# Batch 0's k loaded from two issuing engines, and one tail store moved, in a fused linear-attention and feed-forward kernel

## The chip, the core and the metric

The kernel runs on one core of a Trainium2 chip. The core's engines run their own instruction streams side by side and wait for each other by semaphores. The profile names them PE (TensorE matmul; PEld is its weight load), DVE (VectorE), ACT (ScalarE), POOL (GpSimd) and SP (SyncE, which here only issues transfers). Transfers between HBM and the on-chip memory run on 16 DMA engines. An instruction on SP, ACT or POOL issues a transfer; the profile counts the packets of SyncE's queue as q1 (hardware) and those of POOL's as q0 (software).

The metric is the device time of one execution in microseconds (us), as the median of several runs. The profile is of one execution, and its span runs from the first to the last instruction.

## The reference

Eight batches, eight heads, 576 positions, head size 64, all float32. The first half is linear attention with cosine weights, the second a feed-forward layer on its output.

```python
pos = np.arange(S); theta = np.pi / 2.0 * pos / S
def phi(x, c, s):
    r = np.maximum(x, 0.0)
    return np.concatenate([r * c, r * s], axis=-1)
q_p, k_p = phi(q, cos_w, sin_w), phi(k, cos_w, sin_w)
kv = np.einsum('bhsf,bhsd->bhfd', k_p, v)
z = np.sum(k_p, axis=2)
num = np.einsum('bhsf,bhfd->bhsd', q_p, kv)
den = np.einsum('bhsf,bhf->bhs', q_p, z)[..., None] + 1e-06
attn = num / den
x = attn.transpose(0, 2, 1, 3).reshape(B * S, H * D)     # 4608 x 512
h = x @ w_in                                             # 512 x 2048
g = h * (1.0 / (1.0 + np.exp(-1.702 * h)))
out = g @ w_out                                          # 2048 x 512
```

## The kernel before

The order of every engine's instructions is the order in which the code is written; no scheduler moves them. Each of SP, ACT and POOL works through its own list, so a transfer that has to wait holds up what stands behind it on that engine.

**Start.** For batch 0 the tiles `kf` (k) and `qf` (q) are each loaded in two pieces, along the free dimension: 192 and 384 of the 576 columns of k, 256 and 320 of those of q (L61 to L63). With 128 partitions and four rows each, a piece of k is 512 runs, of 768 bytes in the first and 1536 bytes in the second. All four are issued by SP. POOL writes the index constants (L68 to L73), then copies one element of `kf`'s first piece into a small tile, the gate (L130). That copy has no use but to hold POOL until this piece is there; behind it POOL issues the loads of v as bf16 (`vb`, L132, two of them) and of the first two quarters of w_in (L124).

ACT begins with a table load, the sine and cosine weights (L89, L90) and a second table load with a trial of the gelu (L92). PE runs twelve matmuls on zeros (`idle`, L346) until there is work.

**From k to the feed-forward part.** `trig` (L142 on DVE, L140 on ACT) multiplies the positive part of a 64-column slice j by cosine and sine: two instructions a slice. In k, slices 0 and 1 go to DVE and 2 to ACT (these lie in the first piece); 6, 7, 8 to ACT and 3, 4, 5 to DVE (these lie in the second). Then follow: `ksum`, the sum over positions, on PE (L218); the same trig for q on DVE, ACT and one slice on POOL; turning q on PE (L171) and copying it out (L179, L181); `kv_mm`, the product of k and v (L207), copied out by `kv_evac` (L212); `num_mm` (L230) and its division `num_div` on DVE (L236, L238, L254); turning the quotient `xn` on PE (L274), copied out as `xT` by ACT (L280). With `xT` and `w_in` the first feed-forward matmuls run (L295, from `start_block`, L368).

**Steady state.** For each of eight batches: 64 matmuls of the first layer (L295) with gelu on ACT (L300), then 64 of the second (L332), with the attention of the next batch laid between. Its loads come from SP and POOL while the matmuls run.

**End.** The last 64 rows of each batch are gathered in four tail tiles, t = 4 to 7, each of two batches, and go through both layers at the end (`mm1_tails`, L312; `mm2`, L327). Within `mm2`, ACT copies a result to `ysb` (L336) and one or two stores send it out (L340): a tail tile takes two stores of 64 rows. `last` (L338) chooses the issuing engine. In the last batch, SP issues all but three: both of tile 4 and the first of tile 5 go by POOL.

Of the kernel before, what the change touches and what calls it, by code (L numbers as in the profile page):

```python
# [19 lines left out]
def kernel(  # L20
# [9 lines left out]
    nc = tc.nc  # L30
    B, H, S, D = q.shape
# [20 lines left out]
    def raw(name, dt=F32):  # L52
        return one.tile([128, NI, S], dt, name=name)

    def src_of(src, b, i0=0, i1=NI):
        return src[b, 2 * i0:2 * i1].rearrange("(i hh) (p j) d -> (hh p) i (j d)", hh=2, j=NS)

    qf = one.tile([128, 2560], F32, name="qf")
    kf, vf, vb = raw("kf"), raw("vf"), raw("vb", BF16)
    qf0 = qf[:, 0:NI * S].rearrange("p (i e) -> p i e", i=NI)  # L60
    for t, src, cut in ((kf, k, 192), (qf0, q, 256)):  # L61
        nc.sync.dma_start(out=t[:, :, 0:cut], in_=src_of(src, 0)[:, :, 0:cut])
        nc.sync.dma_start(out=t[:, :, cut:S], in_=src_of(src, 0)[:, :, cut:S])  # L63


    NP = NS + 5
# [251 lines left out]
    def rows(b, t):  # L318

        if t >= 4:  # L320
            return [(64 * u, 64, out_j[w][NS - 1] if w < 2 else out[(w + 1) * S - 64:(w + 1) * S])
                    for u, w in enumerate((2 * (t - 4), 2 * (t - 4) + 1))]
        if b < 2:
            return [(64 * u, 64, out_j[b][2 * t + u]) for u in range(2)]
        return [(0, 128, out[b * S:b * S + 512].rearrange("(p c) d -> c p d", c=4)[t])]

    def mm2(b, t, lo, hi, c0=0, c1=d_model):  # L327
        if lo == 0:
            yp[t, c0] = pmm.tile([128, d_model], F32, name="mm")
        for fc in range(lo, hi):  # L330
            w = gT[fc][:, ts(t, 128)] if t < 4 else gl_t[:, fc, ts(t - 4, 128)]
            nc.tensor.matmul(yp[t, c0][:, c0:c1], w, w_out_sb[:, fc, c0:c1],  # L332
                             start=(fc == 0), stop=(fc == FC - 1))
        if hi == FC:
            ysb = ypool.tile([128, d_model], F32, name="ysb")
            nc.scalar.activation(ysb[:, c0:c1], yp[t, c0][:, c0:c1], AF.Identity)  # L336
            for p0, n, dst in rows(b, t):
                last = b == B - 1 and t != 4 and (t, p0) != (5, 0)  # L338
                eng = nc.sync if last else nc.gpsimd
                eng.dma_start(out=dst[:, c0:c1], in_=ysb[p0:p0 + n, c0:c1])  # L340

# [116 lines left out]
    for t in range(4):  # L458
        mm2(0, t, 0, 4)
    mm2(0, 0, 4, 8)  # L460
    mm2(0, 1, 4, 8)
    ha = at_homes()
    qturn_pe(0, ha[0])
# [117 lines left out]
```

## Time and profile before

| what | us | from |
|---|---|---|
| median of 3 runs (292.34 to 292.56) | 292.51 | times |
| the profiled execution | 292.51 | times |
| its span | 290.8 | profile |
| k, first piece: issue, to landing | 0.79, 3.4 | transfers of `kf` |
| k, second piece: issue, to landing | 1.30, 4.8 | transfers of `kf` |
| q, first piece: issue, to landing | 1.83, 5.6 | transfers of `qf` |
| q, second piece: issue, to landing | 2.38, 7.0 | transfers of `qf` |
| v, first half: issue, to landing | 4.33, 6.2 | transfers of `vb` |
| w_in, first quarter: issue, to landing | 5.98, 10.2 | transfers of `w_in` |
| first feed-forward matmul (L295) starts | 16.20 | timeline |
| last ACT copy of a result ends | 288.04 | timeline |

The profile has a page of summaries (busy times, the chain of work that ended last, groups of instructions, transfers) and views that can be asked of one stretch of time. In a timeline a line has start, duration, engine, line of code, operation, tiles and shapes, and in brackets how long the engine stood before it and what ended that. In the chain of waits a line has start, duration and what was worked on or waited for. A window's line has the window, its length, the busy time of each engine with its instructions, the TensorE clock that was granted, the DMA engines' mean busy share and what they moved in GB/s. A queue's line has packets, MB and the time that its packets took, as a share of 16 engines.

### The profile page before, as it was taken

To read this page: it belongs to the slowest core of one execution; us is meant where nothing else is said; L and a number is where in the kernel's file an instruction comes from. 1 tells how busy PE (TensorE), PEld (TensorE's weight loads), DVE (VectorE), ACT (ScalarE), POOL (GpSimd) and SP (SyncE) were. 2 spreads that over 40 slices of the span, in tenths; PEclk is the share of its full clock that TensorE was granted. 3 is DMA by queue.
4 is the path that set the end of the run, shared out by engine and by line. 5 is a ranking of instruction groups with operands and counts; after the bars stand their busy time and mean duration, and the time that the engine had idled before them with its cause. 6 is when DMAs were issued, how large, how long until landed. Compare 5 with 4: busy or idle time off the path is not lost.

```text
span 290.8 us, 5789 instructions
## 1 busy us (share of the span) xinstructions
PE 284.3 (98%) x2330; PEld 154.8 (53%) x2330; DVE 124.1 (43%) x356; ACT 132.9 (46%) x232; POOL 37.8 (13%) x71
## 2 busy tenths in 40 slices
PE   7989999999999999999999999999999999999995
PEld 2775466755555554555455545554555455544444
DVE  4953645842648363826582567156624200000000
ACT  7957654693156214721463136412651167751111
POOL 6650044101210001001100110011000100002000
PEclk9999999999999999999999999999999999999999
DMA  7999999684689958975699469756975400002322
GB/s 250 244 214 287 372 267 363 172 181 128 126 225 306 220 132 276 260 197 145 225 277 227 122 192 335 184 143 152 379 94 74 117 36 3 0 0 44 87 88 72
DMA packets 67771, 52.48 MB, mean 180 GB/s; under 512 B 47969, under 2 KB 57953, under 8 KB 67745
## 3 DMA queue, kind: packets, MB, share of 16 engines
q1 hardware_dynamic: 60320, 32.52, 45.2%
q0 software_dynamic: 7424, 19.60, 23.6%
q8 instruction: 18, 0.29, 0.4%
q14 instruction: 9, 0.07, 0.1%
HBM read 36.70 MB, written 9.44 MB: 159 GB/s over the span
## 4 chain that ended last, share of the span: by engine, by line
PE 92%; DMA 5%; DVE 1%; POOL 1%; issue 0%; ACT 0%; ACTq 0%
PE mm L332 43%; PE mm L295 38%; PE mm L312 5%; DMA w_in<-in_moe_w_in_dram 3%; PE at L230 3%; PE at L207 3%; DMA kf<-in_k_dram 1%; PE at L171 1%; POOL vb L132 1%; DVE xn L254 0%; PE at L274 0%; DVE inv L238 0%; ACT ysb L336 0%; DVE den L236 0%; POOL gate L130 0%
## 5 line engine op out<-in xcount | busy, mean ns | idle before, releaser
L332 PE MATMUL mm<-w_out_sb,g 128*128 128x512 bf16 (+1 forms) x528 | 117.9, 373 | 0.0
L295 PE MATMUL mm<-xT,w_in 128*128 128x512 bf16 (+1 forms) x608 | 112.9, 345 | 0.2 <-DMA w_in<-in_moe_w_in_dram 0.2
L300 ACT ACTIVATE g<-mm 128x512 bf16<-128x512 f32 x128 | 75.1, 598 | 30.4 <-PE mm L295 30.2
L295 PEld LDWEIGHTS <-w_in 128*128 128x128 bf16 x608 | 61.6, 113 | 49.6 <-DMA w_in<-in_moe_w_in_dram 0.3
L332 PEld LDWEIGHTS <-g 128*128 128x128 bf16 x528 | 48.7, 97 | 49.6
L336 ACT ACTIVATE ysb<-mm 128x512 f32<-128x512 f32 (+1 forms) x37 | 21.7, 586 | 109.7 <-PE mm L332 106.7
L340 POOL DMA_DIRECT2D out_dram<-ysb x39 | 21.2, 547 | 205.6 <-ACT ysb L336 203.6
L142 DVE TENSOR_SCALAR kr<-kf,cosw 128x256 bf16<-128x256 f32 x64 | 22.5, 351 | 30.3 <-DMA kf<-in_k_dram 30.3
L254 DVE TENSOR_TENSOR xn<-at,inv 128x512 bf16<-128x512 f32 x40 | 27.7, 691 | 1.7 <-PE at L230 0.4
L142 DVE TENSOR_SCALAR kr<-kf,sinw 128x256 bf16<-128x256 f32 x64 | 22.6, 354 | 0.0
L236 DVE TENSOR_SCALAR den<-at 128x8 f32<-128x8 f32 x39 | 6.5, 166 | 34.4 <-PE at L230 34.4
L230 PEld LDWEIGHTS <-qT 128*128 128x128 bf16 x320 | 14.6, 97 | 8.1 <-issue 0.8
L212 DVE CAST kvs<-at 128x520 bf16<-128x520 f32 (+1 forms) x9 | 5.7, 635 | 28.9 <-PE at L207 28.9
L230 PE MATMUL at<-kvs,qT 128*128 128x65 bf16 x320 | 15.9, 193 | 0.7 <-ACT xT L280 0.7
L155 DVE TENSOR_SCALAR qn<-qf,sinw 128x512 bf16<-128x512 f32 (+1 forms) x30 | 14.4, 480 | 0.0
L155 DVE TENSOR_SCALAR qn<-qf,cosw 128x512 bf16<-128x512 f32 (+1 forms) x30 | 14.3, 476 | 0.0
L312 PE MATMUL mm<-xt,w_in 128*128 128x512 bf16 x64 | 14.0, 379 | 0.0
L332 PE MATMUL mm<-w_out_sb,gl_t 128*128 128x512 bf16 x64 | 14.0, 379 | 0.0
L313 ACT ACTIVATE gl_t<-mm 128x512 bf16<-128x512 f32 x16 | 9.6, 597 | 4.2 <-PE mm L312 4.2
L312 PEld LDWEIGHTS <-w_in 128*128 128x128 bf16 x64 | 7.2, 113 | 6.6
L207 PEld LDWEIGHTS <-kr 64*128 64x128 bf16 x576 | 9.3, 94 | 2.7 <-issue 2.5
L332 PEld LDWEIGHTS <-gl_t 128*128 128x128 bf16 x64 | 6.3, 98 | 7.5
(63 smaller groups left out, 115.4 us busy)
## 6 DMA issues: line engine op xcount, KB each, us to landing
kf<-in_k_dram SPq DMA_DIRECT2D x5, 1152.0 KB, 6.9
vf<-in_v_dram SPq DMA_DIRECT2D x5, 1152.0 KB, 9.6
qf<-in_q_dram SPq DMA_DIRECT2D x5, 1024.0 KB, 6.2
out_dram<-ysb POOLq DMA_DIRECT2D x20, 256.0 KB, 2.8
out_dram<-ysb POOLq DMA_DIRECT2D x19, 128.0 KB, 4.1
kf<-in_k_dram POOLq DMA_DIRECT2D x2, 1152.0 KB, 11.7
vf<-in_v_dram POOLq DMA_DIRECT2D x2, 1152.0 KB, 16.5
w_in<-in_moe_w_in_dram POOLq DMA_DIRECT2D x4, 512.0 KB, 10.2
```

What stands on the lines that cost most here:

```text
L142: eng.tensor_scalar(o, i, 0.0, w[:, j:j + 1], op0=MAX, op1=MUL)
L155: nc.vector.tensor_scalar(o, i, 0.0, sc, op0=MAX, op1=MUL)
L207: nc.tensor.matmul(st["kv", i][:, hh, ds(col, n)], kr[r, j, i, :], rhs(r, i, j), start=(j == 0), stop=(j == NS - 1))
L230: nc.tensor.matmul(ps[:, h // 4, ds((h % 4) * 65, 65)], qT[:, h, ts(c, 128)], st["kvs"][:, hh, i, 0:65], start=True, stop=True)
L254: nc.vector.tensor_tensor(xn, pv[:, :, :, 0:64], inv.unsqueeze(3).to_broadcast([128, 2, 4, 64]), op=MUL)
L295: nc.tensor.matmul(hp[fc][:, t0:t1], w_in_of(kc, fc), x[b][:, kc, t0:t1], start=(kc == 0), stop=(kc == KC - 1))
L300: nc.scalar.activation(g, hp.pop(fc), AF.Gelu_apprx_sigmoid)
L312: nc.tensor.matmul(hps, w_in_of(kc, fc), xt[:, kc, :], start=(kc == 0), stop=(kc == KC - 1))
L313: nc.scalar.activation(gl_t[:, fc, :], hps, AF.Gelu_apprx_sigmoid)
L332: nc.tensor.matmul(yp[t, c0][:, c0:c1], w, w_out_sb[:, fc, c0:c1], start=(fc == 0), stop=(fc == FC - 1))
L336: nc.scalar.activation(ysb[:, c0:c1], yp[t, c0][:, c0:c1], AF.Identity)
L340: eng.dma_start(out=dst[:, c0:c1], in_=ysb[p0:p0 + n, c0:c1])
```

## The change

Two edits. The loop that loads k and q of batch 0 has an engine beside each pair: the second piece of k is issued by ScalarE (ACT), where it stands ahead of the first table load in that engine's list; the second piece of q and both first pieces stay on SP. And the condition for the stores of the last batch loses its exception, so the first store of tail tile 5 is issued by SP and no longer by POOL. PE and DVE have the same instructions as before, in the same order.

```diff
-    for t, src, cut in ((kf, k, 192), (qf0, q, 256)):
+    for t, src, cut, eng in ((kf, k, 192, nc.scalar), (qf0, q, 256, nc.sync)):
         nc.sync.dma_start(out=t[:, :, 0:cut], in_=src_of(src, 0)[:, :, 0:cut])
-        nc.sync.dma_start(out=t[:, :, cut:S], in_=src_of(src, 0)[:, :, cut:S])
+        eng.dma_start(out=t[:, :, cut:S], in_=src_of(src, 0)[:, :, cut:S])
...
-                last = b == B - 1 and t != 4 and (t, p0) != (5, 0)
+                last = b == B - 1 and t != 4
                 eng = nc.sync if last else nc.gpsimd
                 eng.dma_start(out=dst[:, c0:c1], in_=ysb[p0:p0 + n, c0:c1])
```

## The prediction

> **What bounds the kernel now.** I read the page's busy times first, then the chain of waits in order of time, then the timeline of the first 20 us, then the transfers in short windows.
>
> ```profile
> span 290.8 us, 5789 instructions
> ...
> PE 284.3 (98%) x2330; PEld 154.8 (53%) x2330; DVE 124.1 (43%) x356; ACT 132.9 (46%) x232; POOL 37.8 (13%) x71
> ```
>
> PE is busy for 98% of the span, so time can be won or lost only where PE does filler (the warm-up matmuls of L346) or stands: in the first 19 us, and after the last matmul. The chain of waits shows what the start hangs on:
>
> ```profile
> 4.21 0.18 POOL gate L130
> 4.38 1.59 POOL vb L132 x2
> 5.98 10.17 DMA w_in<-in_moe_w_in_dram
> ```
>
> Ahead of these the chain has k's first piece (L62, on SyncE's queue, issued 0.79, landed 4.16). The first real matmul of the feed-forward part (L295) starts at 16.20, when the first w_in tile has landed. But it has a second condition that came almost as late. The timeline (start, duration, engine):
>
> ```profile
> 4.26 0.35 DVE L142 TENSOR_SCALAR kr<-kf,cosw 128x256 bf16<-128x256 f32 x1 [2.15 <-DMA kf<-in_k_dram]
> ...
> 5.26 0.34 DVE L142 TENSOR_SCALAR kr<-kf,sinw 128x256 bf16<-128x256 f32 x1
> ...
> 6.12 0.51 ACT L140 ACTIVATE kr<-kf,cosw 128x256 bf16<-128x256 f32 x1 [0.97 <-DMA kf<-in_k_dram]
> 6.12 0.35 DVE L142 TENSOR_SCALAR kr<-kf,cosw 128x256 bf16<-128x256 f32 x1 [0.52 <-DMA kf<-in_k_dram]
> ...
> 15.65 0.39 PE L274 MATMUL at<-ident,xn 128*128 128x128 bf16 x4
> ...
> 16.20 1.09 PE L295 MATMUL mm<-xT,w_in 128*128 128x128 bf16 x16 [0.16 <-DMA w_in<-in_moe_w_in_dram]
> ```
>
> PE had ended its turn of xn at 16.04 and stood 0.16 us. So two chains race: the arithmetic from k to xT (16.04) and the w_in load (16.2). DVE uses k's first piece for four operations from 4.26 to 5.60, stands 0.52, and from 6.12, when the second piece is there, is busy almost without a gap until 13.2, each result feeding the next. ACT has the same shape with a gap of 0.97.
>
> The windows (columns: window, its length, busy of PE, PEld, DVE, ACT, POOL, clock, DMA share, GB/s) say how k came:
>
> ```profile
> 1.90:2.40 0.50, 0.50 (x2) 0.15 (x1) 0.12 (x2) 0.49 (x3) 0.38 (x1) 1.00 0.81 72
> 2.40:2.90 0.50, 0.50 (x2) 0.15 (x1) 0.00 (x0) 0.48 (x2) 0.00 (x0) 1.00 0.68 152
> 2.90:4.20 1.30, 1.30 (x4) 0.44 (x3) 0.00 (x0) 1.10 (x2) 0.00 (x0) 1.00 1.09 385
> 4.20:6.10 1.90, 1.77 (x19) 0.93 (x17) 1.34 (x4) 0.91 (x2) 1.89 (x4) 1.00 1.07 396
> 6.10:8.60 2.50, 1.80 (x26) 1.12 (x25) 2.48 (x9) 2.48 (x7) 1.42 (x2) 1.00 1.08 390
> 8.60:16.20 7.60, 6.64 (x158) 5.19 (x157) 6.75 (x21) 5.98 (x13) 6.49 (x9) 1.00 1.23 209
> ```
>
> After a slow first microsecond SyncE's queue alone keeps all 16 DMA engines full, 385 to 396 GB/s, until k and q (2.36 MB) are through at 8.6. Adding up the rates, k's first 393 kB had passed by 3.63 and landed at 4.16, all 1180 kB by 5.63, landed 6.1: about half a microsecond from last byte to release.
>
> **The change, part by part.**
>
> *ScalarE issues k's second piece.* SP's issues of the kind took 0.46 to 0.51 us here (one later k load 1.52). It stands ahead of ACT's first table load, which so moves from 0.79 to about 1.28; cosw, ready at 2.50 now, is ready near 3.0 (4.0 at the longest issue), and nothing asks for it before k lands at 4.16. ACT's own start on k moves from 4.24 to 4.5, covered by the later landing below. Cost nothing; without that cover, 0.5.
>
> *SP issues q 0.5 us earlier* (1.83 to 1.30, 2.38 to 1.83). Worth nothing by itself: the DMA engines are full until 8.6, and the order of bytes decides.
>
> *k's two pieces are now asked for at the same time.* This is the step that costs. Today they come one after the other: every packet before 3.0 is of 768 bytes, the first piece's. From two queues they can take turns. The nearest rows are POOL's queue (q0) beside SyncE's (q1), first in 8.5 to 9.0, then in 88 to 89 (packets, MB, share):
>
> ```profile
> q0 software_dynamic: 65, 0.07, 86.6%
> q1 hardware_dynamic: 59, 0.06, 34.5%
> ```
> ```profile
> q1 hardware_dynamic: 88, 0.20, 51.1%
> q0 software_dynamic: 71, 0.20, 50.9%
> ```
>
> When both run, they alternate nearly packet for packet. Each piece of k is 128 x 4 = 512 packets (768 and 1536 bytes), so taking turns both end together, with the whole 1180 kB: the first piece lands at 6.1 instead of 4.16, the second at 6.1 as now. DVE then does ten kr operations from 6.1 where it did six from 6.12. The first four take 1.34 (4.26 to 5.60), so today's work is as if ten had started at 6.12 - 1.34 = 4.78: DVE's chain is late by 1.32. ACT's shift is smaller (its first two took 0.91). DVE's stream stays packed, so xT is late by the same; minus the 0.16 in which PE now waits for w_in: +1.16. If the turns go by bytes instead, the first piece lands at 5.15 and the second, sharing with q's first piece, at 7.1: DVE late by 0.98, sum +0.82. If ACT's piece goes wholly first, DVE, which takes the first piece first, is as late as with turns.
>
> What could be won is the slow first microsecond: 112 kB moved between 1.9 and 2.9 where 390 could. No row shows two queues starting at once. Bounds: no gain, or the whole start-up, 0.7 us; I take 0.3, as if each queue starts at the row's rate (224 kB instead of 112). Both landings are then 5.8, DVE late by 1.02, PE by 0.86.
>
> [...]
>
> *What follows POOL's gate.* The gate (L130) waits for k's first piece, so vb and w_in are issued some 1.6 us later: vb near 6.0, w_in at 7.6. Cover: those bytes could not move anyway. vb was issued at 4.33 and two packets of POOL's queue passed before 8.5, when q was through; a POOL store near the end had its first packet 1.1 us after its issue (264.34 to 265.45). Issued at 6.0, vb is ready at 7.1, before 8.3 to 8.6. From there the queue runs without a gap at about 209 GB/s, so w_in lands at 16.15 or 0.3 sooner. Without the cover the cost is a rival below. The late POOL trig of q (L142) has 1.6 us to spare before its turn at 13.6.
>
> *The tail store.* The first store of tile 5 moves from POOL (0.53 us at 267.8) to SP, where one more issue of 0.33 to 0.59 ends near 268.5; SP's next store is ready at 270.96. Its semaphore wait is for a transfer of the stage before, long landed. The end hangs on the last ACT copy at 287.66 and its store: nothing; without the 2.4 us of cover, 0.5.
>
> **Sum.** Profiled execution: 292.51, its span 290.8 and 1.7 around it; the median of the runs is the same 292.51. 292.51 + 0.86 = 293.4. PE is full from 19 us on, so nothing later gives it back. The likeliest case's own range is 292.9 (0.7 of start-up won) to 293.7 (none).
>
> **Rivals.**
> 1. *The first piece still goes first; not slower.* For it: a queue with work in hand is not interrupted. vb waited from 4.33 to 8.4, and a POOL store issued at 82.58 behind a k load of 80.63 landed only after 6.5 us. If SP's packets are at the DMA engines first, k lands at 4.16 and 6.1 as now: 292.5. If the start-up is also 0.3 to 0.5 shorter, DVE's 0.52 gap closes, w_in follows as q drains earlier, and PE starts up to 0.5 sooner: 292.0. It decides as soon as the first piece lands before 4.78 while the second is no later than 6.1. Against it: both issues leave at about 0.79, so neither has work in hand.
> 2. *The w_in load becomes the bound.* If the 10.17 us from issue to landing were latency that moves with the gate, w_in would land 1.6 to 1.9 later and PE with it: 294.1 to 294.4. Against it: the empty POOL queue until 8.4.
> 3. *The second queue changes nothing:* ScalarE's issue comes first in its program, but if its packets only join when SP's first piece is through, the order of bytes is the old one and the time is 292.5. Against it: SP's own issue had packets 1.1 us later (0.79 to 1.9), and ACT stood free from 0.79 as well.
>
> **How the numbers follow.** Taking turns, or ScalarE's piece first: 0.62, of it 0.55 slower than 0.2% (0.585 us; about what a measurement of this kernel can tell from no change) and 0.07 within. First piece first: 0.25, of it 0.15 within and 0.10 faster. w_in: 0.08, slower. The rest 0.05, spread 0.02 faster, 0.02 within, 0.01 slower. That makes 0.12 faster, 0.24 the same, 0.64 slower. Range 292.1 to 294.0: it takes in most of rival 1 and the upper end of the turns, and leaves out the best of rival 1 and rival 2.
>
> **What would show it.** Right: k's first piece lands at 5 to 6.1; DVE's first kr operation starts there, without a gap before its fifth; the gap of PE before L295 is put down to the xn turn, not to w_in; w_in's time from issue to landing shrinks from 10.2 to below 9; L295 starts near 17.1. Wrong: a first piece at 4.2 (rival 1), POOL's queue standing idle after 8.6 (rival 2), or PE gaps behind the tail.

## The result, and the profile after

The changed kernel takes 294.68 us as the median of 6 runs (293.62 to 294.99), the kernel before 292.36 (292.22 to 292.56, 6 runs): a ratio of 1.007, 95% interval 1.0059 to 1.0081, or 2.3 us more. Its runs fall into two groups with nothing between: four at 294.64 to 294.99, in which TensorE's mean granted clock is 0.992 to 0.994, and two at 293.62 and 293.66 with a clock of 1.000. The median lies in the first group. The profiled execution (294.72, span 293.0) is one of the first group.

The heads of the page, TensorE's clock in 40 slices of the span, and two lines of the chain of waits:

```profile
span 293.0 us, 5752 instructions
...
PE 283.2 (97%) x2294; PEld 155.3 (53%) x2330; DVE 124.6 (43%) x356; ACT 132.8 (45%) x232; POOL 37.1 (13%) x70
...
PEclk9799999999999999999999999999999999999998
```
```profile
0.79 4.93 DMA kf<-in_k_dram
5.83 2.13 DVE kr L142 x6
```

k's first piece now lands 4.93 us after its issue, not 3.4, and DVE's work on it has entered the chain that ended last. In the timeline, lines that answer to those of the prediction, and the matmul that PE waited to start:

```profile
5.78 0.18 POOL L130 COPY gate<-kf 1x1 f32<-1x1 f32 x1 [3.50 <-DMA kf<-in_k_dram]
5.81 0.51 ACT L140 ACTIVATE kr<-kf,cosw 128x256 bf16<-128x256 f32 x1 [1.29 <-DMA kf<-in_k_dram]
5.83 0.35 DVE L142 TENSOR_SCALAR kr<-kf,cosw 128x256 bf16<-128x256 f32 x1 [3.71 <-DMA kf<-in_k_dram]
...
6.50 0.25 PE L218 MATMUL mm<-sel,kr 128*128 128x2 bf16 x4 [0.78 <-DVE kr L142]
...
7.22 0.35 PE L218 MATMUL mm<-sel,kr 128*128 128x2 bf16 x8 [0.47 <-DVE kr L142]
...
8.63 0.59 PE L346 MATMUL mm<-warm 128*128 128x512 bf16 x1
...
14.08 1.02 ACT L179 ACTIVATE qT<-mm 128x1024 bf16<-128x1024 bf16 x1 [1.77 <-PE mm L171]
...
14.26 0.17 DVE L236 TENSOR_SCALAR den<-mm 128x8 f32<-128x8 f32 x1 [0.55 <-PE mm L244]
...
17.99 1.06 PE L295 MATMUL mm<-xT,w_in 128*128 128x128 bf16 x16
```

Three things are to be seen. DVE has no gap before its fifth operation any more; it starts 1.57 us later (5.83 for 4.26). PE stands in two long pieces at 5.7 to 7.2, and from 8.2 on its matmuls are longer (a filler on zeros takes 0.59 us where it took 0.38). And DVE and ACT, which led PE before, now wait for it; the chain of waits runs through PE's work from 8.0 on, where before it ran through the w_in load. The windows show the clock that was granted:

```profile
8.00:8.20 0.20, 0.20 (x5) 0.20 (x6) 0.20 (x1) 0.20 (x1) 0.20 (x1) 0.93 1.03 384
8.20:8.40 0.20, 0.20 (x4) 0.01 (x1) 0.20 (x2) 0.20 (x2) 0.20 (x2) 0.50 1.05 390
...
11.20:11.40 0.20, 0.20 (x4) 0.20 (x3) 0.20 (x2) 0.20 (x1) 0.20 (x1) 0.50 1.24 213
11.40:11.60 0.20, 0.20 (x5) 0.20 (x4) 0.20 (x1) 0.20 (x2) 0.20 (x1) 0.54 1.22 203
```

It is 0.50 from about 8.17 to 11.58, 3.4 us (worked out from the two mixed windows, 0.93 and 0.54).

L295 starts 1.79 us later than before, and that delay is carried unchanged to the end: the last ACT copy ends at 289.81 for 288.04, 1.77 later. The span, however, is 2.2 longer. From the last ACT copy to the end it now takes 3.19 us, before 2.76 (spans are given to 0.1 us), though the last store lands 1.8 us after its issue in both. So there are two places to explain, the first 18 us and the last 3.

### The profile page after: what moved, and what is told of

The parts are those of the page before. It is cut to its first block, busy times and chain, and to the rows that moved or that the text cites. A ratio compares the mean times of both kernels' runs of the same rounds, so it can differ in the third digit from the quotient of the medians.

```text
span 293.0 us, 5752 instructions
## 1 busy us (share of the span) xinstructions
PE 283.2 (97%) x2294; PEld 155.3 (53%) x2330; DVE 124.6 (43%) x356; ACT 132.8 (45%) x232; POOL 37.1 (13%) x70
## 4 chain that ended last, share of the span: by engine, by line
PE 93%; DVE 2%; DMA 2%; ACT 2%; issue 1%; ACTq 0%; DVEq 0%
PE mm L332 42%; PE mm L295 36%; PE mm L312 5%; PE at L207 3%; PE at L230 3%; DMA kf<-in_k_dram 2%; ACT g L300 1%; PE mm L346 1%; PE mm L171 1%; DVE kr L142 1%; DVE xn L254 1%; PE at L171 1%; PE at L274 1%; PE mm L218 0%; ACT xT L280 0%
## 5 line engine op out<-in xcount | busy, mean ns | idle before, releaser
L332 PE MATMUL mm<-w_out_sb,g 128*128 128x512 bf16 (+1 forms) x505 | 116.2, 372 | 1.4 <-issue 0.3
L295 PE MATMUL mm<-xT,w_in 128*128 128x512 bf16 (+1 forms) x599 | 112.4, 345 | 0.5
L295 PEld LDWEIGHTS <-w_in 128*128 128x128 bf16 x608 | 61.7, 113 | 49.3
L340 POOL DMA_DIRECT2D out_dram<-ysb x38 | 20.4, 538 | 203.5 <-ACT ysb L336 203.4
L142 DVE TENSOR_SCALAR kr<-kf,sinw 128x256 bf16<-128x256 f32 x64 | 22.0, 345 | 0.0
```

Source lines behind the costliest of these rows:

```text
L142: eng.tensor_scalar(o, i, 0.0, w[:, j:j + 1], op0=MAX, op1=MUL)
L295: nc.tensor.matmul(hp[fc][:, t0:t1], w_in_of(kc, fc), x[b][:, kc, t0:t1], start=(kc == 0), stop=(kc == KC - 1))
```

## The experiments

All times are medians, with the kernel before run beside them on the same chip (292.29 in the first set, 292.30 in the second, 292.53 in the third).

**act_only: the first edit alone.**

```diff
-                last = b == B - 1 and t != 4
+                last = b == B - 1 and t != 4 and (t, p0) != (5, 0)
```

> Only the first edit: k's second piece on ScalarE's queue; the first store of tile 5 goes by POOL as before. If the whole loss comes from the first edit, the time is that of the change: about 293.6 where the clock stays at 1.000 and 294.6 to 295.0 where it drops to half near 8 us, and the span ends about 1.4 us after the last store has landed (1.36 in the change, 0.9 before). If the tail store on SP makes the longer end, the span ends 0.9 us after the last landing again and both times are 0.4 lower.

Measured: 293.24, ratio 1.0041 (1.0024 to 1.0058). Six runs at 293.09 to 293.36 with a clock of 0.998 to 1.000, two at 294.30 and 294.94 with 0.993 and 0.994. The last copy ends at 290.48 of a span of 293.2: 2.7 us, as before. The first of the two expectations, that all loss is in the first edit, was wrong; the second held for the undisturbed runs. What stays is +0.9 in the undisturbed runs and more where the clock drops.

**tail_only: the second edit alone** (the exception for tile 5 taken out of the kernel before).

> Only the second edit: the first store of tile 5 on SP, all loads as before. If the tail store costs nothing: 292.4, ratio 1.000, the span ends 0.9 us after the last landing. If it makes the longer end of the change: 292.8, ending 1.4 us after it.

Measured: 292.66, ratio 1.0016 (1.0008 to 1.0025), and 3.2 us from the last copy to the end. The times are 0.37 above the kernel before. The one store, which should have cost nothing, makes the longer end.

**act_store: the same store by ScalarE in place of POOL, loads as before.**

```diff
-                eng = nc.sync if last else nc.gpsimd
+                eng = nc.sync if last else nc.scalar if b == B - 1 and (t, p0) == (5, 0) else nc.gpsimd
```

> The kernel before with one difference: the first store of tile 5 is issued by ScalarE (near 267.5) in place of POOL. Loads and start as before. If the mere use of a second hardware queue costs time at the end of the execution: the span is 0.3 to 0.5 longer, 292.8, and it ends about 1.4 us after the last landing, L295 first at 16.2. If the longer end belongs to the start of the change or is chance: 292.4, ending 0.9 us after the last landing.

Measured: 292.75, ratio 1.0017 (1.0006 to 1.0028), 3.19 us from the last copy to the end. (L295 starts at 16.70 in this profile and not at 16.2; the six profiles with the old loads and the old fillers have it anywhere from 15.84 to 16.70.) By itself the longer end looks like a price of the second queue, but act_only uses that queue and ends in 2.7. What tail_only, act_store and the change share is one more transfer on the hardware queues (SP's and ScalarE's together). act_only has as many as before. In the built program each such transfer gets one of eight completion semaphores in turn, and a store first waits for the earlier transfer on its own. The last store of the kernel before, and of the change:

```
95 L340 DMACopy out_dram<-ysb 128x256 [waits DMAHW7_49,Activation_49]
95 L340 DMACopy out_dram<-ysb 128x256 [waits DMAHW0_49,Activation_49]
```

One transfer more moves the last store from the last of the eight semaphores to the first. The built program ends, behind the last store, with SyncE waiting for the eight one after the other, 0 first and 7 last (L576). The trace has these waits. From the last landing until SyncE goes on, the kernel before has one left, the change eight:

```profile
L576 SPq EVENT_SEMAPHORE  x1: 28/28/28, 289.9 to 289.9; - x1
```
```profile
L576 SPq EVENT_SEMAPHORE  x8: 28/28/28, 291.7 to 292.1; - x8
```

The seven more start some 0.06 us apart, 0.4 us in all.

**end_mid, end_six, end_one: the last store on other semaphores,** by moving tail stores between SP and POOL in the kernel before.

```diff
-                last = b == B - 1 and t != 4 and (t, p0) != (5, 0)
+                last = b == B - 1 and t not in (4, 5, 6) and (t, p0) != (7, 0)   # end_mid
+                last = b == B - 1 and t not in (4, 5)                            # end_six
+                last = b == B - 1 and (t, p0) != (4, 0)                          # end_one
```

> The kernel before with four more tail stores issued by POOL: both of tile 5, both of tile 6 and the first of tile 7. The number of transfers on the hardware queues falls by four, so with eight completion semaphores given out in turn the last store of all sits on the fourth (index 3) and not on the last (index 7). If the end of the program waits for the eight in order, each after the last landing costing its share, the span ends 2.74 + 4/7 x 0.45 = 3.0 us after the last ACT copy, time 292.55. If only index 7 is short, 3.2. If what matters is that POOL issues the store, or that SP issues one more, it stays at 2.75 or gets shorter: 292.3.

> The kernel before with one more tail store by POOL (the second of tile 5), so the last store of all sits on index 6 of the eight semaphores. If each semaphore still to be asked after the last landing costs about 0.06 us: from the last ACT copy to the end of the span 2.8 (index 7 gave 2.72 to 2.76, index 3 3.08, index 0 3.17 to 3.20). If the order of asking is another one, anything up to 3.2.

> The kernel before with two more tail stores by SP (the first of tile 5, the second of tile 4), so the last store of all sits on index 1. If the semaphores are asked in order: 3.1 to 3.15 from the last ACT copy to the end of the span, a little under the 3.2 of index 0. If the end grows with the number of stores that SP issues: more than 3.2.

From the last ACT copy to the end of the span (spans are given to 0.1 us):

| index of the last store's semaphore | SyncE's waits from the last landing on | us | kernels |
|---|---|---|---|
| 7 | 1 | 2.72 to 2.76 | before, act_only, act_fill, no_fill, same_order |
| 6 | 2 | 2.81 | end_six |
| 3 | 5 | 3.08 | end_mid |
| 1 | 7 | 3.15 | end_one |
| 0 | 8 | 3.17 to 3.20 | the change, tail_only, act_store, after_fill |

The end shortens as the index rises, whichever engine issues the moved stores and however many SP issues. After the last landing the program still waits for that store's semaphore and for the later ones, one after the other, some 0.06 us each. (end_mid was expected at 3.0.) The times of these three kernels (end_mid 292.61, 1.0013, 1.0001 to 1.0024; end_six 292.34, 0.9995, 0.9983 to 1.0006; end_one 292.68, 1.0002, 0.9986 to 1.0018) are too coarse to show such steps.

**after_fill: the change with more filler at the start.**

```diff
-    w = idle(12)
+    w = idle(18)
```

> The change with 18 warm-up matmuls on zeros in place of 12, so PE is busy until about 7.0 us and not 5.7. If PE's stand between 5.7 and 8 us is what halves its clock, and the clock what parts the runs of 294.7 from those of 293.6: clock 1.000 in every run, all times 293.5 to 293.8, L295 first near 16.9 to 17.1. If the clock drops for another reason (the DMA or DVE load of the first 8 us), times are as in the change, 293.6 to 295.0 in two groups. If the six added matmuls (about 1.3 us) hold up the sum of k: a still later L295, above 18.

Measured: 293.65, ratio 1.0047 (1.0035 to 1.0059); six runs at 293.56 to 293.87, clock 0.997 to 1.000, L295 at 16.82. The stretch from 5.7 to 8.2 us in the change (first line) and with the filler (second):

```profile
5.70:8.20 2.50, 1.06 (x19) 0.66 (x19) 2.38 (x7) 2.39 (x6) 2.42 (x4) 0.99 1.08 390
```
```profile
5.70:8.20 2.50, 2.50 (x26) 1.24 (x24) 2.50 (x8) 2.50 (x7) 2.50 (x4) 1.00 1.07 388
```

DVE, ACT and the DMA engines do nearly the same in both; PE is busy for 1.06 us of the 2.5 in the one, for all of it in the other. With six useless matmuls more, no run has the clock of 0.992 to 0.994. L295 starts 1.17 us earlier than in the change's profile; a part of that is not the clock, since in this execution k's first piece also landed 0.3 us earlier (DVE starts on it at 5.54, not 5.83).

**act_fill: the first edit alone, with the filler.** Both edits above together.

> The first edit alone (the first store of tile 5 by POOL as before) with 18 warm-up matmuls in place of 12. If the loss is three separate things (start +0.9, clock drop in some runs, end +0.45), only the first is left: clock 1.000 in every run, 293.2, all runs within 0.4, and the span ends 2.75 us after the last ACT copy as before. If the long end goes with the fuller start or with ScalarE's queue: 293.6, 3.2 us after the last copy.

Measured: 293.42, ratio 1.0039 (1.0024 to 1.0053), all five runs at 293.35 to 293.50, 2.73 us from the last copy to the end, L295 at 17.07. In act_only's profile, which is of a run at 0.994, DVE starts on k's first piece at 5.79, here at 5.78; L295 starts there at 18.34, 1.27 later, with a clock of 0.50 from 9.66 on. What is left here is the cost of the late first piece by itself, 1.1 us; without the filler act_only's undisturbed runs gave 0.9. Whether the longer filler costs the 0.2 between them stays open.

**no_fill: the kernel before without the fillers between the sums of k.**

```diff
     for j in (3, 6, 4, 7, 5):
-        idle(1, w)
         ksum(j)
-    idle(1, w)
     ksum(8)
```

> The kernel before without the six filler matmuls between the sums of k (zeros on zeros, no result). Loads as before. If PE's stand in the window from 5.7 to 9 us is enough to halve the clock: clock below 1.000 in some or all runs, and those about 0.5 to 1.2 us longer, 292.8 to 293.5, the rest 292.3. If the clock drops only together with the change's loads: clock 1.000 throughout and 292.2 to 292.3.

Measured: 293.50, ratio 1.0041 (1.0026 to 1.0056), all four runs at 293.39 to 293.64 with a clock of 0.994. k lands as before (3.4 and 4.9 us after issue), yet L295 starts at 17.25:

```profile
9.20:9.40 0.20, 0.20 (x6) 0.16 (x4) 0.19 (x2) 0.20 (x1) 0.00 (x0) 0.75 1.24 213
9.40:12.40 3.00, 2.78 (x47) 2.24 (x48) 2.76 (x6) 2.50 (x7) 2.60 (x4) 0.50 1.22 206
...
12.60:12.80 0.20, 0.20 (x8) 0.13 (x3) 0.00 (x0) 0.00 (x0) 0.20 (x1) 0.72 1.32 220
```

The same 3.4 us at a clock of 0.50, with the old loads. So the drop needs nothing of the change but the thinner work on PE, and it costs 1.2 us here.

**same_order: both queues, the old order of bytes.**

```diff
-    for t, src, cut in ((kf, k, 192), (qf0, q, 256)):
-        nc.sync.dma_start(out=t[:, :, 0:cut], in_=src_of(src, 0)[:, :, 0:cut])
-        nc.sync.dma_start(out=t[:, :, cut:S], in_=src_of(src, 0)[:, :, cut:S])
+    for c0, c1 in ((0, 192), (192, S)):
+        for i0, eng in ((0, nc.sync), (2, nc.scalar)):
+            eng.dma_start(out=kf[:, i0:i0 + 2, c0:c1], in_=src_of(k, 0, i0, i0 + 2)[:, :, c0:c1])
+    for c0, c1 in ((0, 256), (256, S)):
+        nc.sync.dma_start(out=qf0[:, :, c0:c1], in_=src_of(q, 0)[:, :, c0:c1])
...
-                last = b == B - 1 and t != 4 and (t, p0) != (5, 0)
+                last = b == B - 1 and t not in (4, 5) and (t, p0) != (6, 0)
```

> The kernel before with k cut over the two queues another way: SP and ScalarE each load one half of the rows of the first piece, then each one half of the second; q on SP as before; two tail stores go from SP to POOL so that the last store keeps its semaphore (index 7). Both queues now carry the bytes in the old order. If taking turns between the pieces is what made the first one late: all of the first piece lands at 4.0 to 4.3, L295 starts at 16.0 to 16.3, time 292.2 to 292.5. If using a second queue makes the loads slow by itself: first piece after 5, time 293 or more. If two queues shorten the start-up by the 0.3 that the prediction took: first piece near 3.9, time 292.0.

Measured: 292.70, ratio 1.0013 (1.0004 to 1.0023). All of the first piece is there at about 4.1 (DVE starts at 4.19), the second near 6.3, L295 at 16.46. ScalarE's queue carries half of each piece, and the first piece is on time; so the order of the bytes is what made it late. From 2 to 4 us this kernel moved 174 and 375 GB/s, where one queue moved 138 and 386 (means of 2 to 3 and 3 to 4 us): 0.02 MB more, or 0.06 us. Two queues shorten the start-up by next to nothing. The time is 0.2 above what was expected for this case. What the 0.4 us above the kernel before consists of stays open; L295 is 0.26 later, which is inside the 15.84 to 16.70 of the six profiles with the old loads and fillers.

## Why the prediction was wrong

The direction was right and the step that was priced came out near its price, in part by luck. The time was too low because of two steps that failed: the prediction had no price for what PE's stand does to TensorE's clock (measured: 1.2 us in the runs where it dropped), and it priced the moved tail store at nothing (0.4). Without the drop of the clock the time is 293.64 (the two runs at a clock of 1.000), inside the range of 292.1 to 294.0; with it, outside.

**k's first piece, taking turns: right in the end, its size by errors that cancelled.** Forecast: landing at 5.8, +0.86. Measured: landing at 5.72, DVE from 5.83, +0.9 (act_only, undisturbed runs) to +1.1 (act_fill). The queues did take turns, but not from the start (q1 is SP's, q10 ScalarE's; first 2 to 3 us, then 3 to 4):

```profile
q1 hardware_dynamic: 153, 0.12, 66.1%
q10 hardware_dynamic: 4, 0.01, 1.6%
```
```profile
q10 hardware_dynamic: 135, 0.21, 57.7%
q1 hardware_dynamic: 192, 0.15, 45.0%
```

Both transfers were issued at 0.79, yet ScalarE's queue had moved 4 packets by 3.0, when SP's had moved 160 of the 512 of the first piece. That head start, which the forecast did not have, brought the first piece forward; then the turns favoured the small packets (192 to 135), and from 4 to 5 us they were nearly even (165 to 178). Why ScalarE's queue starts later stays open. It is also why the 0.3 us of start-up that the forecast took off did not come: the change moved 124 and 355 GB/s from 2 to 4 us, less than the 138 and 386 of one queue. The landing lies between the two bounds, by packets (6.1) and by bytes (5.15). The second piece landed at 6.46, not 5.8, and no engine had to wait for it: DVE asked for it at 7.08, ACT at 6.62.

**ScalarE's issue, free: right.** It took 0.47; the cosine weights were ready at 3.01, long before 5.72.

**POOL's gate, hidden: right.** v and w_in were issued 1.6 us later, as forecast, and w_in landed 7.3 us after its issue, at 14.9. Rival 2 is out. L295 waited for xT. That w_in came earlier than the 16.15 of the profile before is not shown to be the change's doing: with the old loads it landed 8.5 to 8.6 us after its issue, at 14.5 to 14.7, in end_mid, end_six and end_one, and L295 did not wait for it there. The close race of two chains that the prediction read was that of one execution.

**The tail store, free: wrong.** The prediction looked at the store's issue and at the wait ahead of it, not at what follows the last landing. One transfer more on the hardware queues moved the last store from semaphore 7 to 0, and the span ends 0.43 later. In times: 293.64 (the change's two runs at 1.000) less 293.2 (act_only's) is 0.4; tail_only has 0.37 alone.

**PE's stand, priced at nothing: wrong, and the largest term.** The prediction saw that time can be lost where PE does filler or stands, but it reckoned only how late the work comes. Before, the sums of k and the fillers between them followed the warm-up matmuls almost at once, and PE was busy for 1.80 of the 2.5 us from 5.7 to 8.2:

```profile
5.70:8.20 2.50, 1.80 (x29) 1.10 (x29) 2.08 (x7) 2.08 (x6) 1.82 (x3) 1.00 1.08 391
```

In the change it was busy for 1.06, and in four of six runs the mean clock fell (0.992 to 0.994); the profile of one of them shows 0.50 for 3.4 us, and in it DVE and ACT wait for PE's sums and turns. That costs 1.2 (294.8 less 293.64), as no_fill does without the change.

It strikes only some runs, six of fourteen of the change and act_only. In the three profiles with a drop (the change, act_only, no_fill) the clock falls to 0.50 at 8.17, 9.66 and 9.30, each time for 3.413 us, and falls again after PE's last matmul, in each 283.306 us after the first fall; that is 83 times 3.4133. In the kernel before, the warm-up matmuls start 0.43 us apart up to 4.21 and 0.22 apart from there (the profile gives the clock as 1.00 all along), and from 4.20 to the clock's fall at 290.918 it is 286.72 us, 84 times 3.4133. An estimate from these distances: in these executions the clock changed only at steps of 3.413 us, which lay differently against the start of the kernel in each. That this is what parts the runs is not shown, since only one run of each kernel has a trace.

The sum, then: 0.9 for the late first piece, 0.4 at the end, 1.2 for the clock in four of six runs, together 2.5; those four lie 2.3 to 2.6 above the kernel before.

## What to carry to other kernels

Where one queue already fills the DMA engines (386 to 402 GB/s from 3 to 8 us here), a second one added no bandwidth (355 to 395). It only changed the order of the bytes, and a piece that was cut small to arrive early lost its place. The six filler matmuls between the sums of k (granted clock 0.994 without them in no_fill, 0.998 or more with them) were worth 1.2 us here, as much as work on the critical path: when the work that such fillers bridge moves, their number has to be looked at anew. A transfer added or taken away can shift which semaphore the last store gets, so compare the time from the last instruction to the end of the span as well.

## What was not expected of the hardware

PE had not stood for long when its clock fell: its longest stand between the warm-up matmuls and the drop in the change was 0.78 us. In no_fill the profile has it busy for 2.91 us of the 4 from 5 to 9 us, in the kernel before for 3.18. The first ran at 0.50 from 9.3 to 12.7 in its profile and at a mean of 0.994 in all four runs; the second had 0.998 or more in every run beside the experiments. But less busy time, as the profile gives it, did not always go with a drop. Of the two stretches of 3.41 us shown here the first (act_only) ended in the drop at 9.66. The second (tail_only; its end lies 81 times 3.4133 us ahead of the clock's fall at 293.210) did not end in one, with less of PE:

```profile
6.24:9.65 3.41, 2.75 (x39) 1.42 (x39) 3.41 (x11) 3.41 (x10) 2.79 (x4) 1.00 1.12 347
```
```profile
13.32:16.73 3.41, 2.34 (x45) 1.72 (x43) 2.69 (x9) 2.13 (x3) 3.20 (x6) 1.00 1.24 207
```

The first is mostly sums of k with two columns, and fillers; the second, from 13.83 on, has wider matmuls (65 to 512 columns). No run here shows what in PE's work brings the drop. And the place of the last store's semaphore in a row of eight is worth 0.43 us at the end of the profiled executions.
